# FFT mixing followed by a ReGLU FFN on one core: batch 0 loaded by casting DMAs and folded inside the matmuls of stage 1, with the weights loaded behind it

## The chip, the cores and the metric

The kernel runs on one core of one Trainium2 chip. The metric is the device time of one execution in microseconds (us), the median of several executions. A profiled execution leaves a trace; its span is about 2 us shorter than the device time of the same execution (645.1 against 646.91 us in the kernel before). A program on one core has no second core to compare with, so its clock is read from its own trace.

Engines: PE is TensorE (matmul), PEld its weight load, DVE is VectorE, ACT is ScalarE, POOL is GpSimd, SP the engine that issues most of the DMAs. SBUF and PSUM are the two memories in which the kernel places its tiles: matmuls write to the tiles in PSUM, all other tiles are in SBUF. The granted clock is the share of its full clock at which PE was allowed to run. A dummy matmul is one whose result nobody uses; it only keeps PE busy.

## The reference

```python
X = np.fft.fft(x, axis=1)                 # x: (8, 3008, 256), f32
X = np.fft.fft(X, axis=2).real            # 24064 tokens of 256 features
gate = np.maximum(X @ w_gate, 0.0)        # w_gate, w_val: (256, 1536)
val  = X @ w_val
out  = (gate * val) @ w_out               # w_out: (1536, 256)
```

## The kernel before

The sequence length is split as 3008 = 94 x 32. Stage 1 is a DFT of length 94 over the partitions, one matmul group for each of 16 values `jj`. A shuffle through DRAM turns the result around, and stage 2 is a DFT of length 32 that yields `pq` (two halves, `cs` = 0 and 1) for a block of 512 columns. The feature DFT is never run on the data. It is put into the weights: `pair_w` adds and subtracts the two halves of a weight chunk, and `fold_w` multiplies them in f32 with a table of cosines and sines (`cd`) to give `wc`, `ws` and a scaled copy `wm`. There are twelve folds in all: three column chunks `n`, two weights `i`, two tables `cs`.

```python
def pair_w(n, i, eng):
    lo, hi, up = (wst[i, n, c] for c in range(3))
    eng.tensor_tensor(up, lo, hi, op=ALU.add)
    eng.tensor_tensor(lo, lo, hi, op=ALU.subtract)

def fold_w(n, i, cs, evac="act"):
    ...                                                      # two f32 matmul pairs into ps
    if cs == 0:
        plain(wc[i][:, sl_], ps[:])
    else:
        plain(ws[i][:, sl_], ps[:])
        nc.scalar.activation(wm[i][:, sl_], ps[:], ACTF.Copy, scale=s2[:])
```

After that come 288 steps (8 batches x 3 blocks x 12 columns of 128 of the hidden dimension). A step computes the gate from `pq`, `wc` and `ws`, the value, and their product. The first twelve steps have no output matmuls yet. They therefore have room on PE, and some folds sit between them. The output matmuls of a block run beside the steps of the next block.

Batch 0 comes as f32 through SP, DVE and POOL fold it (`fold_first`: sum and difference of each feature with its mirror feature), and stage 1 then needs two matmuls of 256 columns for a `jj`. The order of the program after the tables is also the order in which each engine works in these traces (the `pq` copy ran behind `pair_w(1, 1)` at 38.26 us in the changed kernel, and ahead of it, at 33.65, when an experiment exchanged the two calls):

```python
for r in (0, 24):
    fold_first(r, 8, ALU.add, dve)
...                                                          # more sums on DVE, differences on POOL
for c0, c1, ev in ((1, 4, "aaa"), (4, 6, "aa"), (6, 8, "ad"), (0, 1, "a")):
    for c in range(c0, c1):
        stage1(0, c, "act" if ev[c - c0] == "a" else "dve")  # 4 matmuls and a copy out of PSUM
    shuffle_out(0, c0, c1)
load_w(1, (1,))
for blk in range(NBLK):
    shuffle_in(0, 4 * blk, 4 * blk + 4)
load_w(2)
...
pair_w(0, 0, dve)
for cs, off in enumerate((o0, o1)):                          # stage-2 table m2: DVE chain and a sine on ACT
    if cs:
        pair_w(0, 1, dve)
        fold_w(0, 0, 0)
        fold_w(0, 0, 1)
    ...
fold_w(0, 1, 0)
fold_w(0, 1, 1)
...
pair_w(1, 0, pl)
pair_w(1, 1, dve)
fold_w(1, 0, 0, "act")
fold_w(1, 0, 1, "act")
...
stage2(0, 0, 0, "act")
rotate(0)
fold_w(1, 1, 0, "act")
stage2(0, 0, 1, "dve")                                       # its copy on DVE releases the first full gate
```

## Time and profile before

| | |
|---|---|
| time | 647.8 us (647.26 to 647.83) |
| span of the profiled execution | 645.1 us |
| PE busy over the span | 96% |
| last stage-1 copy ends | 24.56 us |
| stage 2 starts | 33.26 us |
| first full gate (matmul of `ws` with the second half of `pq`) | 37.37 us |
| first output matmul | 65.09 us |

The page shows where PE is not full. Its second part cuts the span into 40 slices of 16.1 us; a digit is the busy share of PE in tenths, and in the second line the granted clock of PE in tenths of full speed:

```profile
PE   6878999899999999999999999999999999999995
PEclk9699999999999999999999999999999999999999
```

Apart from the eighth and the last slice (8 and 5), only the first four have room, and the second one ran at a low clock. This is the stretch that the change touches. The chain of waits, whose lines give start, length and what, has one piece for the folding of batch 0:

```profile
7.93 10.42 POOL eo L139 x6
```

The windows view by stage follows. The columns are the stretch in us, its length, then busy us and (instructions) of PE, PEld, DVE, ACT and POOL, then the granted clock, the DMA share and GB/s. The four stretches are stage 1 (here from the end of the dummy matmuls ahead of it, after the change from its first matmul), last stage-1 copy to stage 2, stage 2 to the first full gate, and the twelve steps without output:

```profile
9.70:24.57 14.87, 8.35 (x36) 6.09 (x38) 13.60 (x26) 8.15 (x13) 12.93 (x19) 0.65 0.73 220
24.57:33.26 8.69, 7.67 (x25) 2.78 (x21) 7.63 (x19) 4.25 (x9) 3.57 (x5) 0.81 0.80 240
33.26:37.37 4.11, 2.13 (x16) 0.81 (x16) 0.70 (x3) 2.48 (x6) 3.80 (x4) 1.00 1.09 308
37.37:65.09 27.72, 24.29 (x125) 9.23 (x125) 19.35 (x32) 15.52 (x29) 20.21 (x29) 1.00 0.66 123
```

In stage 1, DVE and POOL work for 13.6 and 12.9 of 14.9 us, PE for 8.4 us and at a mean clock of 0.65. The timeline from the end of stage 1 to the first full gate (start, us, engine, line, operation, out<-in, shapes, count, and in brackets the idle time before it and its releaser):

```profile
23.98 0.58 ACT L193 CAST t<-ps 96x512 bf16<-96x512 f32 x1 [2.07 <-PE ps L181]
...
28.95 4.37 PE L282 MATMUL psw<-wst,cd 128*64 128x512 f32 x16 [1.02 <-DVE wst L275]
...
32.26 0.32 POOL L457 COPY seen<-t 1x1 bf16<-1x1 bf16 x1 [4.78 <-DMA t<-Td]
...
33.26 0.40 PE L225 MATMUL ps<-m,t 128*128 128x128 bf16 x4
...
37.37 0.37 PE L518 MATMUL G<-pq,ws 128*128 128x496 bf16 x1 [0.57 <-DVE pq L232]
```

The POOL copy at 32.26 is a marker: it reads one element of the shuffled data and so shows when the shuffle has landed. Stage 2 starts a microsecond later. The last line is the first full gate; PE waited 0.57 us for the `pq` copy.

### The profile page before, as it was taken

The numbers are of one execution on the slowest core, as the hardware profiler recorded it, in microseconds if no ns is written. First come the engines' busy times: TensorE is split into PE (matmuls) and PEld (weight loads), VectorE is DVE, ScalarE is ACT, GpSimd is POOL, SyncE is SP. The second block draws the span as 40 slices with busy tenths as digits, with TensorE's granted clock in tenths as the row PEclk, the third lists the DMA queues.
The fourth block names the chain that finished last, engine by engine and source line by source line (L and its number), as shares of the span: only waits on it lengthen the run. The fifth ranks groups of instructions, "written<-read, shape, count | busy, mean of one in ns | idle before, by whom it ended". The sixth has DMA issues, their size and how long they took to land.

```text
span 645.1 us, 11866 instructions
## 1 busy us (share of the span) xinstructions
PE 618.7 (96%) x4231; PEld 410.4 (64%) x4231; DVE 549.3 (85%) x642; ACT 444.7 (69%) x846; POOL 521.9 (81%) x436
## 2 busy tenths in 40 slices
PE   6878999899999999999999999999999999999995
PEld 3423666666666666666666666676666666666664
DVE  9847888788988988988988897888988898899991
ACT  5455687667677767677777776777677777766660
POOL 9559989999999999999998999898555555556661
PEclk9699999999999999999999999999999999999999
DMA  9694753562735284344723555211512133212114
GB/s 248 197 242 68 173 147 83 153 161 67 207 83 137 43 234 103 106 102 114 195 65 87 121 142 150 59 33 37 156 51 60 46 93 93 67 33 65 32 39 92
DMA packets 35635, 70.72 MB, mean 110 GB/s; under 512 B 6124, under 2 KB 23508, under 8 KB 32244
## 3 DMA queue, kind: packets, MB, share of 16 engines
q1 hardware_dynamic: 32152, 57.92, 34.2%
q0 software_dynamic: 3120, 11.80, 8.0%
q8 instruction: 33, 0.54, 0.4%
q10 hardware_dynamic: 304, 0.25, 0.2%
q14 instruction: 26, 0.21, 0.1%
HBM read 39.77 MB, written 30.96 MB: 110 GB/s over the span
## 4 chain that ended last, share of the span: by engine, by line
PE 82%; DMA 5%; POOL 5%; DVE 3%; ACT 2%; issue 1%; SPq 1%; ACTq 0%; POOLq 0%; DVEq 0%
PE po L581 35%; PE V L532 17%; PE G L524 8%; PE G L518 8%; PE G L517 8%; DMA t<-Td 2%; DMA Td<-t 2%; PE ps L183 2%; POOL eo L139 2%; PE ps L225 1%; PE psw L282 1%; DVE E L539 1%; POOL h L552 1%; SPq L632 1%; DVE h L545 1%
## 5 line engine op out<-in xcount | busy, mean ns | idle before, releaser
L552 POOL TENSOR_TENSOR h<-gm,E 128x992 bf16<-128x992 f32 (+1 forms) x138 | 319.9, 2318 | 87.2 <-DVE E L559 51.7
L581 PE MATMUL po<-wo,h 128*128 128x256 bf16 (+2 forms) x2304 | 326.0, 272 | 0.0
L581 PEld LDWEIGHTS <-h 128*128 128x128 bf16 (+2 forms) x2304 | 231.7, 103 | 106.1
L526 ACT ACTIVATE gm<-G 128x496 f32<-128x496 f32 (+1 forms) x288 | 170.3, 591 | 101.0 <-PE G L524 95.9
L545 DVE TENSOR_TENSOR h<-gs,V 128x1024 bf16<-128x1024 f32 (+3 forms) x150 | 173.7, 1158 | 54.9 <-PE V L532 40.5
L539 DVE SCALAR_TENSOR_TENSOR E<-nb,af,V 128x496 f32<-128x496 bf16 (+1 forms) x276 | 190.2, 730 | 12.3 <-POOL h L552 5.6
L519 ACT ACTIVATE gs<-G 128x497 f32<-128x497 f32 (+2 forms) x288 | 169.7, 589 | 26.2 <-PE G L518 24.1
L559 DVE SCALAR_TENSOR_TENSOR E<-E,V 128x992 f32<-128x992 f32 (+1 forms) x138 | 164.3, 1190 | 0.0
L524 PE MATMUL G<-pq,wm 128*128 128x496 bf16 (+1 forms) x288 | 107.9, 375 | 2.3 <-ACT gs L519 2.2
L518 PE MATMUL G<-pq,ws 128*128 128x497 bf16 (+2 forms) x288 | 107.9, 375 | 0.6 <-DVE pq L232 0.6
L517 PE MATMUL G<-pq,wc 128*128 128x497 bf16 (+2 forms) x288 | 107.9, 375 | 0.0
L532 PE MATMUL V<-pq,ws 128*128 128x497 bf16 (+2 forms) x288 | 85.4, 374 | 3.5 <-DVE E L539 3.4
L532 PE MATMUL V<-pq,wc 128*128 128x497 bf16 (+2 forms) x288 | 85.5, 375 | 0.0
L594 ACT COPY os<-po 128x512 f32<-128x512 f32 x63 | 36.9, 586 | 17.6 <-PE po L581 17.0
L518 PEld LDWEIGHTS <-ws 128*128 128x128 bf16 x288 | 28.2, 98 | 32.6
L193 ACT CAST t<-ps 96x512 bf16<-96x512 f32 x63 | 36.6, 581 | 8.7 <-PE ps L181 6.7
L532 PEld LDWEIGHTS <-wc 128*128 128x128 bf16 x288 | 27.7, 98 | 22.5 <-issue 3.9
L517 PEld LDWEIGHTS <-wc 128*128 128x128 bf16 x288 | 28.2, 98 | 20.3 <-issue 2.9
L110 POOL TENSOR_TENSOR eo<-xla 94x254 bf16<-94x254 f32 x56 | 39.9, 722 | 1.0
L107 POOL TENSOR_TENSOR xla<-xla,xha 94x510 f32<-94x510 f32 x28 | 35.4, 1264 | 2.2
L110 POOL TENSOR_TENSOR eo<-xlb 94x254 bf16<-94x254 f32 (+1 forms) x42 | 33.7, 813 | 0.7
L532 PEld LDWEIGHTS <-ws 128*128 128x128 bf16 x288 | 26.5, 97 | 9.7 <-issue 6.3
(125 smaller groups left out, 380.9 us busy)
## 6 DMA issues: line engine op xcount, KB each, us to landing
out_dram<-os SPq DMA_DIRECT2D x126, 128.0 KB
out_dram<-os SPq DMA_DIRECT2D x86, 64.0 KB
Td<-t SPq DMA_DIRECT2D x7, 768.0 KB
t<-Td SPq DMA_DIRECT2D x7, 768.0 KB
xla<-in_x_dram SPq DMA_DIRECT2D x7, 720.0 KB
xlb<-in_x_dram SPq DMA_DIRECT2D x7, 640.0 KB
nb<-Nd SPq DMA_DIRECT2D x24, 128.0 KB
out_dram<-os SPq DMA_DIRECT2D x39, 48.0 KB
```

The source lines that it names most:

```text
L110: yield eng.tensor_tensor(e1[:, :, o:o + H - 1], x1[:, :, 1:H], free(x1, D - 1, [D, n], [-1, H - 1]), op=op)
L517: nc.tensor.matmul(G[:, ds], lhsT=wc[0][:, fs], rhs=pq[:, 0, ds], start=True, stop=False)
L518: nc.tensor.matmul(G[:, ds], lhsT=ws[0][:, fs], rhs=pq[:, 1, ds], start=False, stop=True)
L519: nc.scalar.activation(pair(t, "gs")[:, t % 2, ds], G[:, ds], ACTF.Relu)
L524: nc.tensor.matmul(G[:, cols], lhsT=wm[0][:, f * 128:(f + 1) * 128], rhs=pqt[b, blk][:, 1, cols], start=False, stop=True, skip_group_check ...
L526: nc.scalar.activation(pair(t, "gm")[:, t % 2, cols], G[:, cols], ACTF.Relu)
L532: nc.tensor.matmul(pair(t, "V")[:, t % 2, cs], lhsT=w[:, f * 128:(f + 1) * 128], rhs=pqt[b, blk][:, min(k, 1), cs], start=(k == 0), stop=( ...
L539: nc.vector.scalar_tensor_tensor(pair(t, "E")[:, t % 2, cols], nbt[b, blk][:, cols], af[:, f:f + 1], pair(t, "V")[:, t % 2, cols], op0=ALU ...
L545: nc.vector.tensor_tensor(pair(t, "h")[:, k, 0, 0:ds.stop - ds.start], pair(t, "gs")[:, k, ds], pair(t, "V")[:, k, ds], op=ALU.mult)
L552: eng.tensor_tensor(free(pair(t, "h")[:], 1024 * (t % 2) + 512 + w - 1, [1024, n], [-1, w]), pair(t, "gm")[:, k, cols], val[:, k, cols], o ...
L559: nc.vector.scalar_tensor_tensor(E[:, :, cols], E[:, :, cols], 2.0, V[:, :, cols], op0=ALU.mult, op1=ALU.subtract)
L581: nc.tensor.matmul(po[0:m, i, :], lhsT=pair(t - f + ff, "h")[:, ff % 2, sg, g * 128:g * 128 + m], rhs=wo[:, ff, :], start=(ff == 0), stop= ...
```

## The change

Its intent is to take the folding of batch 0 off DVE and POOL. The loads of x go through POOL's queue and cast to bf16. The upper rows are gathered in reversed order by an index tile. Stage 1 reads each row forward and reversed and does the folding by accumulation in PSUM: eight matmuls of about 128 columns for a `jj` instead of two of 256. The weight loads start when x has landed. Along with this, tables, folds and copies were reordered. The diff, cut to its core:

```diff
-        for r in FIRST:
-            nc.sync.dma_start(out=t[r // JH][:, r % JH:r % JH + 4, :], ...)   # f32
+            nc.gpsimd.dma_start(out=dst, in_=view(x, r * D, ...))              # f32 -> bf16, lower rows
+            nc.gpsimd.indirect_dma_start(out=dst..., in_offset=...ixf...)      # f32 -> bf16, upper rows reversed
...
-                nc.tensor.matmul(o, lhsT=w1[:, jj, :], rhs=eo[:, jj, :], start=True, stop=False)
-                nc.tensor.matmul(o, lhsT=w1h[:, NB // 2 - jj, :], rhs=eh[:, NB // 2 - jj, :], start=False, stop=True)
+                r0, r1 = (free(v, D - 1, [-1, H - 1]) for v in (x0, x1))       # reversed reads
+                run(o, [(0, H + 1, ce[0], x0[:, 0:H + 1]), (1, H, ce[0], r0),
+                        (1, H, ce[1], r1), (0, H + 1, ce[1], x1[:, 0:H + 1])])
+                run(o, [(H + 1, D, up[0], x0[:, 1:H]), (H + 1, D, up[1], flip[0]),
+                        (H + 1, D, dn[0], r0), (H + 1, D, dn[1], flip[1])])
...
-            nc.scalar.activation(wm[i][:, sl_], ps[:], ACTF.Copy, scale=s2[:])
+            nc.vector.tensor_scalar(wm[i][:, sl_], ws[i][:, sl_], scalar1=s2[:], scalar2=None, op0=ALU.mult)
...
-        (fold_first calls on DVE and POOL)
+        (stage-2 table m2: two chains on DVE with a sine on ACT each, now here)
+        for c0, c1, idle in ((1, 4, 2), (4, 6, 2), (6, 8, 0), (0, 1, 8)):
+            for c in range(c0, c1):
+                stage1(0, c, ("act", "dve")[k % 2])
+            ...
+            warm(idle)                                                         # dummy matmuls
+        for i in range(2):
+            pair_w(0, i, dve)
+            fold_w(0, i, 0, "act")
+            fold_w(0, i, 1, "act")
         pair_w(1, 0, pl)
-        pair_w(1, 1, dve)
-        fold_w(1, 0, 0, "act")
-        fold_w(1, 0, 1, "act")
         ...                                                                    # loads of x of batch 1 and of w_out
+        pair_w(1, 1, dve)
     stage2(0, 0, 0, "act")
     rotate(0)
-    fold_w(1, 1, 0, "act")
     stage2(0, 0, 1, "dve")
...
-    at(0, fold_w, 1, 1, 1, "dve")
     for k in range(4):
-        at(3 + k, fold_w, 2, k // 2, k % 2, "dve" if k % 2 else "act")
+        at(1 + k // 2, fold_w, 1, k // 2, k % 2)
+        at(4 + k, fold_w, 2, k // 2, k % 2)
```

`at(t, ...)` puts work into step t. Before, seven folds run ahead of the steps and five in them; after, four run ahead and eight in them.

## The prediction

> **What bounds it now.** The page has PE busy 96% of the 645.1 us span; the chain of waits gives PE 82%. In the windows view PE is busy 20.0 of 20 us in 80–100 us, and the change does not touch that part. Only the start can move: in the chain the first output matmul stands at 65 us. From timeline and chain:
> - 0–7.9 us: tables on POOL, DVE and ACT while x streams (265 GB/s, last x packet near 14.7).
> - 7.9–18.4: POOL folds batch 0 (10.4 us in the chain).
> - Stage 1 ends with its last copy at 24.57. PE idled from 9.7 to 13.6 but for one matmul, and the granted clock was 0.50 in 15–25: a 256-column matmul took 0.21 us, not 0.11. [...]
> - 24.6–33.3: shuffle through DRAM (landed 32.3) beside six weight folds (1.06 us each at full clock) on PE; stage 2 starts at 33.26, a seventh fold follows, and the first gate matmul that needs both halves runs at 37.37.
> - 37.4–64.8: twelve steps, 1.8 us each without a weight fold and 2.4–2.6 with one.

> **What the change does.** Removes: 24 us of folding of batch 0 (10.6 POOL, 13.3 DVE), the second sine table, three weight folds (3.2 us) before the steps, and the 0.69 us ACT scaling after each fold (now a bf16 DVE op). Adds: stage 1 becomes 128 matmuls of about 128 columns. Four such with new weights took 0.22 us in stage 2, so 7.0 us at full clock, 14 at half (before: 34 matmuls, 7.3 at half). x comes by POOL's queue[...]. A POOL issue took 0.9–1.6 us here, its first packet came 2–5 us after its start, against 1.0 on the sync queue. Casting itself looked free: w_out's cast packets read 1 KB in 60 ns, 270 GB/s over 16 engines. Moves: weight loads behind x; eight weight folds instead of five into the twelve steps.

> **Estimate.** x lands in order: the first two loads near 10 us, the last near 16–17. Stage-1 tables are ready by 9. But the stage-2 sines precede the first stage-1 copy on ACT; their DVE chain (about 25 small ops) ends near 16, and PSUM holds four of eight stage-1 groups until then. The second half of stage 1 runs from 16.5 to 20–23.5, by the clock: last copy about 21.5 (-3). Stage 2 then waits for the shuffle (about 7): 28.3 (-5). First full gate: 30.7 (-6.5), as no fold stands between. Three more folds in the steps give back 1.5–2. Net -4.8, all at the start.

> Predicted 643 us, 80% range 638 to 647.5; faster by over 2%: 3%, within 2%: 95%, slower by over 2%: 2%.

> **What would show it.** Last stage-1 copy at 20–23.5; first full gate at 29–33; the steps in 28–30 us; first output matmul near 60; the stretch after it unchanged within 1 us; clock above 0.5 through most of 10–20.

> **What would make it wrong.** POOL's descriptors late[...], so that x lands after 18; reversed bf16 reads slowing PE (no such read is in this trace); half clock through stage 1 (+3.5 us); the steps with two folds costing over 3.5 us; w_out or batch 1 arriving too late for an earlier loop.

-6.5 us at the first full gate and 1.5 to 2 us given back in the steps make the net -4.8. Of its figures for POOL's queue, the first one is wider in the whole trace of the kernel before: there the first packet came 1.7 to 6.9 us after the start of a POOL issue.

## The result, and the profile after

The changed kernel took 653.8 us (652.86 to 655.09, four runs) against 647.77 us of the kernel before (647.26 to 647.83, four runs): a ratio of 1.0096, with a 95% interval of 1.0076 to 1.0117. It is slower by about 1%, and above the predicted range. A ratio here and below is the mean time of one kernel's runs over the mean of the other's of the same rounds, so it is not quite the ratio of the medians quoted.

| profiled execution | before | after | length of the stretch before | after | predicted for it |
|---|---|---|---|---|---|
| last stage-1 copy ends | 24.56 | 23.25 | 24.56 | 23.25 | 21.5 |
| stage 2 starts | 33.26 | 34.47 | 8.70 | 11.22 | 6.8 |
| first full gate | 37.37 | 38.99 | 4.11 | 4.52 | 2.4 |
| first output matmul | 65.09 | 69.39 | 27.72 | 30.40 | 29.5 |
| end of the span | 645.13 | 651.08 | 580.04 | 581.69 | 580.0 |

(The predicted 29.5 is the old 27.7 and the middle of "1.5–2".) Stage 1 gained 1.3 us, not 3. Each later stretch became longer: by 2.5, 0.4, 2.7 and 1.65 us. The same two lines of the page, after, with slices of 16.3 us:

```profile
PE   7779999899999999999999999999999999999994
PEclk9879999899999999999999999999999999999998
```

The second slice now has a better clock (8 instead of 6), but the third fell from 9 to 7, and a slice further on (the eighth) to 8. The windows view after, for the same four stretches:

```profile
8.81:23.25 14.44, 10.63 (x136) 9.44 (x137) 8.42 (x34) 4.95 (x15) 3.64 (x17) 0.88 0.59 151
23.25:34.47 11.22, 7.89 (x22) 1.96 (x20) 4.94 (x5) 1.76 (x3) 6.51 (x6) 0.85 0.91 297
34.47:38.99 4.52, 1.02 (x12) 0.61 (x12) 3.71 (x5) 1.19 (x3) 4.44 (x4) 0.85 1.06 225
38.99:69.39 30.40, 29.20 (x137) 10.40 (x138) 19.82 (x34) 17.04 (x32) 24.65 (x36) 0.91 0.53 101
```

The first line shows that the aim was met: DVE and POOL fell from 13.6 and 12.9 us to 8.4 and 3.6. Yet the stretch is as long as before. In the second line PE has four folds of 1.06 us to do, where it had six, and takes 11.22 us for them. In the third, PE works 1.02 of 4.52 us. Nothing there is short of engine time, so something is waiting. The timeline after shows for what, first in stage 1:

```profile
14.10 0.31 ACT L40 ACTIVATE sv<-q 128x128 f32<-128x128 f32 x1 [2.08 <-DVE q L39]
...
15.87 0.31 ACT L40 ACTIVATE sv<-q 128x128 f32<-128x128 f32 x1 [1.47 <-DVE q L39]
16.09 1.05 ACT L192 CAST t<-ps 96x512 bf16<-96x512 f32 x2
...
16.42 1.28 DVE L194 CAST t<-ps 96x512 bf16<-96x512 f32 x2
16.70 0.27 PE L162 MATMUL ps<-lo,w 94*96 94x129 bf16 x2 [3.70 <-ACT t L192]
```

The two `sv` lines are the sines of the stage-2 table. They stand ahead of the first stage-1 copy in ACT's order and wait for their chain on DVE. PE had filled the PSUM buffers that it may use and stood idle for 3.70 us, until ACT's first copy freed one. x was not the reason: its last cast packet arrived at 13.17 us (14.74 us before, as f32). The next piece is the folds:

```profile
24.18 2.44 PE L279 MATMUL psw<-wst,cd 128*64 128x512 f32 x8
...
26.66 0.59 ACT L286 CAST ws<-psw 128x512 bf16<-128x512 f32 x1 [0.27 <-PE psw L279]
27.28 0.35 DVE L287 TENSOR_SCALAR wm<-ws,s 128x512 bf16<-128x512 bf16 x1 [2.70 <-ACT ws L286]
27.35 1.40 POOL L272 TENSOR_TENSOR wst<-wst 128x512 f32<-128x512 f32 x1 [13.17 <-DMA wst<-in_moe_w_gate_dram]
27.55 1.75 DVE L272 TENSOR_TENSOR wst<-wst 128x512 f32<-128x512 f32 x1
...
29.35 1.07 PE L279 MATMUL psw<-wst,cd 128*64 128x512 f32 x2 [2.73 <-DVE wst L272]
30.48 0.53 POOL L453 COPY seen<-t 1x1 bf16<-1x1 bf16 x1
31.02 3.52 PE L279 MATMUL psw<-wst,cd 128*64 128x512 f32 x6 [0.60 <-DVE wst L273]
...
34.47 0.40 PE L224 MATMUL ps<-m,t 128*128 128x128 bf16 x4
```

The shuffle had landed by 30.48, but stage 2 started at 34.47, behind the folds in PE's order. After the second fold PE waits 2.73 us for the add of `pair_w(0, 1)`. DVE could have done that add long before, but it stands behind the scaling `wm`, and the scaling waits for ACT's copy of `ws`, which waits for PE's second fold. When DVE comes to it, POOL has just begun its own pair, and DVE's add of the same shape takes 1.75 us instead of 0.68. The last six fold matmuls then take 3.52 us, at half clock (0.50 granted from 30.83 to 34.24). The third stretch:

```profile
35.98 0.68 DVE L272 TENSOR_TENSOR wst<-wst 128x512 f32<-128x512 f32 x1
36.69 1.64 DVE L273 TENSOR_TENSOR wst<-wst 128x512 f32<-128x512 f32 x1
38.26 0.68 DVE L231 CAST pq<-ps 128x512 bf16<-128x512 f32 x1
38.99 0.57 PE L514 MATMUL G<-pq,ws 128*128 128x496 bf16 x1 [2.57 <-DVE pq L231]
```

PE had finished stage 2 at 36.2. DVE first worked through `pair_w(1, 1)`, which nobody needed yet, and only then copied `pq`. The gate waited 2.57 us for that copy.

Last, the late part. In the waits view (engine, line, waited for: us in total, times, longest) the line of `E` for the start of a block reads before (105 to 130 us), then after (109 to 136 us):

```profile
DVE E L539 <- DMA nb<-Nd: 2.7, 1, 2.7
```

```profile
DVE E L535 <- DMA nb<-Nd: 3.3, 1, 3.3
```

Both kernels wait there for a row that goes through DRAM at the end of stage 2 of batch 1. After the change the wait is followed by a stretch at half clock (122.99 to 126.40), which the trace of before has not. Between steps 11 and 36 the two traces run at a constant distance of 4.3 us; at steps 37 to 40 it grows by 2.4 us, falls back to 4.89 by the last step, and what follows the last step's gate (the last output matmuls and the stores) adds 1.06 us.

The granted clock is a part of all this. Up to the last matmul, the stretches at half clock in these two traces last 3.41 us or multiples of it (17.18–20.59, 30.83–34.24, 37.66–44.48, 122.99–126.40; before there was one, 14.22–27.88). In the 3.41 us ahead of each of them PE was not idle: it was busy for 14, 31, 37 and 35% of that time, and for 24% ahead of the one before the change.

### The profile page after: what moved, and what is told of

It reads as the page before. It is cut to its first block, busy times and chain, and to the rows that moved or that the text cites. A ratio compares the mean times of both kernels' runs of the same rounds, so it can differ in the third digit from the quotient of the medians.

```text
span 651.1 us, 12004 instructions
## 1 busy us (share of the span) xinstructions
PE 623.4 (96%) x4294; PEld 413.9 (64%) x4327; DVE 541.1 (83%) x645; ACT 439.5 (68%) x841; POOL 511.9 (79%) x431
## 4 chain that ended last, share of the span: by engine, by line
PE 74%; POOL 11%; issue 3%; DVE 2%; DMA 2%; ACT 1%; POOLq 0%; ACTq 0%; DVEq 0%
PE po L577 31%; PE V L528 15%; PE G L513 8%; PE G L520 8%; PE G L514 8%; POOL h L548 5%; POOL eo L110 2%; PE ps L162 2%; POOL xlb L107 1%; PE psw L279 1%; DMA t<-Td 1%; PE ps L224 1%; DVE E L535 1%; POOL xla L107 1%; DMA nb<-Nd 1%
## 5 line engine op out<-in xcount | busy, mean ns | idle before, releaser
L528 PE MATMUL V<-pq,ws 128*128 128x496 bf16 (+2 forms) x276 | 83.7, 378 | 3.6 <-DVE E L535 3.6
L528 PE MATMUL V<-pq,wc 128*128 128x496 bf16 (+2 forms) x270 | 82.5, 378 | 0.0
L514 PEld LDWEIGHTS <-ws 128*128 128x128 bf16 x288 | 28.3, 98 | 33.0 <-issue 0.5
L192 ACT CAST t<-ps 96x512 bf16<-96x512 f32 x60 | 34.8, 582 | 6.0 <-PE ps L162 4.1
L520 PEld LDWEIGHTS <-wm 128*128 128x128 bf16 x288 | 28.2, 98 | 7.8 <-issue 5.1
```

The costliest lines, as they stand in the source:

```text
L514: nc.tensor.matmul(G[:, ds], lhsT=ws[0][:, fs], rhs=pq[:, 1, ds], start=False, stop=True)
L520: nc.tensor.matmul(G[:, cols], lhsT=wm[0][:, f * 128:(f + 1) * 128], rhs=pqt[b, blk][:, 1, cols], start=False, stop=True, skip_group_check ...
L528: nc.tensor.matmul(pair(t, "V")[:, t % 2, cs], lhsT=w[:, f * 128:(f + 1) * 128], rhs=pqt[b, blk][:, min(k, 1), cs], start=(k == 0), stop=( ...
```

## The experiments

The theory was: (A) the new order makes PE wait in three places, namely the stage-1 copies behind the sines, the second pair behind the first weight's scaling, and the `pq` copy behind `pair_w(1, 1)`. The rivals: (B) it is only the clock, which falls in gaps and would be kept by dummy matmuls; (C) it is contention of DVE with POOL; (D) it is the x path itself, that is casting loads, reversed reads, or the weights' late arrival. The expectations of the first three experiments use other letters: there B is x and the weights arriving late, and C is the cost of steps with two weight folds.

The kernels ran in three sets on three chips. Each set has its own runs of the kernel before (medians 648.4, 647.62 and 648.46 us), and the ratios are to those. The changed kernel ran again only in the third set, so in the other two it can be compared only by way of the kernel before. All kernels gave correct results.

A caution for reading the milestones: the changed kernel's profiled executions differ by up to 2 us in where stage 1 ends (23.25 here, 25.28 in a later one), and the stretch at half clock lies differently there (17.18 to 20.59 us here; in the later one the matmuls of 127 columns took 0.31 us, as in that stretch, from 16.75 to 24.24 us, instead of the 0.22 at full clock). The lengths between milestones are steadier: 11.22, 4.52 and 30.40 us in the first, 11.42, 4.49 and 30.61 us in the later one.

### The `pq` copy ahead of the pair

```diff
-        pair_w(1, 1, dve)
     ...
     stage2(0, 0, 1, "dve")
+    pair_w(1, 1, nc.vector)
```

> The changed kernel with one DVE op pair moved: the add and subtract of the second slice of w_val stand behind the copy of the first stage-2 sine half (pq) instead of ahead of it. Theory A (order on DVE): that pair held DVE from 35.98 to 38.33 us while PE had stage 2 done at 36.2, so the first full gate comes about 2.3 us earlier (36.5 instead of 38.99), PE loses less clock, time 650 to 651.5. Rival B (x by POOL's queue and the weights behind it land too late) and rival C (steps with two weight folds are what costs): no change, 653 to 654.

Measured: 649.18 us (645.67 to 650.14, four runs), ratio 1.0015 [0.9998, 1.0032]; a little better than expected. From stage 2 to the gate it took 2.53 us instead of 4.52. The timeline:

```profile
33.65 0.69 DVE L231 CAST pq<-ps 128x512 bf16<-128x512 f32 x1 [0.70 <-issue]
...
34.39 0.37 PE L514 MATMUL G<-pq,ws 128*128 128x496 bf16 x1 [0.57 <-DVE pq L231]
```

DVE copies `pq` as soon as stage 2 ends, and PE waits 0.57 us, as it did in the kernel before. This place is worth 2 us, and it is shown. The milestone itself moved more (34.39 against 38.99). The rest is not plainly from the edit, for it lies ahead of the moved pair: in this execution DVE's add of `pair_w(0, 1)`, begun 0.25 us ahead of POOL's, took 0.69 us and POOL's 1.56, and the last six fold matmuls ran at full clock in 1.93 us.

### Both pairs ahead of the four folds

```diff
         for i in range(2):
             pair_w(0, i, dve)
+        for i in range(2):
             fold_w(0, i, 0, "act")
             fold_w(0, i, 1, "act")
```

> The changed kernel with both add/subtract pairs of the first weight slices put ahead of the four weight folds on DVE. Theory A: the third fold no longer waits behind the bf16 scaling of the second and behind POOL; PE runs the four folds without its gap of 2.7 us (26.6 to 29.35) and at full clock, stage 2 begins at 30 to 31 (shuffle landing) instead of 34.47, time 649 to 651. Rival B (w_val has not landed before 27 us): the pair just waits at its new place, stage 2 within 0.5 us of 34.5, time 653 to 654.

Measured: 647.28 us (646.8 to 647.77, four runs), ratio 0.9983 [0.9966, 1.0]; better than expected. The timeline:

```profile
24.92 4.16 PE L279 MATMUL psw<-wst,cd 128*64 128x512 f32 x16
...
33.19 0.69 DVE L272 TENSOR_TENSOR wst<-wst 128x512 f32<-128x512 f32 x1 [2.21 <-DMA wst<-in_moe_w_val_dram]
...
35.28 0.57 PE L515 MATMUL G<-pq,ws 128*128 128x496 bf16 x1 [2.14 <-DVE pq L231]
```

The 16 matmuls of the four folds now run in one piece. From the end of stage 1 to stage 2 it took 5.76 us instead of 11.22, and stage 2 starts 0.66 us behind the last fold. The order of DVE was the cause of the gap between the folds. Part of the gain was given back at the next place: DVE came early to `pair_w(1, 1)`, whose weights had not arrived, and held the `pq` copy behind that DMA (stage 2 to gate 5.54 us).

### Both edits

```diff
 (both diffs above)
```

> Both moves. Theory A: first full gate at 32 to 34, time 646 to 648.5, so the loss against the kernel before is gone; the steps from first full gate to first output matmul stay near 30 us or fall to 28 by the clock. Rival C (two folds in a step cost what was lost): the first gate comes earlier but the twelve steps grow, time stays above 651.

Measured: 646.48 us (645.2 to 647.12, four runs), ratio 0.9967 [0.995, 0.9984]. The first full gate is at 33.12 us and the first output matmul at 62.77. With two reorderings of DVE, and nothing else, the change is no longer slower than the kernel before. The steps took 29.65 us, as long as the prediction had them, so the steps with two weight folds are not the unforeseen loss.

### POOL's pair later

```diff
-        pair_w(1, 0, pl)
         pl.tensor_copy(seen[:, 0:1], ...)
         ...                                  # loads of x of batch 1, issue of w_out
+        pair_w(1, 0, pl)
         pair_w(1, 1, dve)
```

> The changed kernel with POOL's add/subtract of the second w_gate slice moved behind the issue of w_out, so that it no longer runs beside DVE's pair of w_val at 27.5 to 31. Theory A, part contention: DVE's two ops fall from 1.75 and 1.64 us to 0.69 each, the third fold starts at 28.3 to 28.9 instead of 29.35 and the fold group ends 1.5 to 2.5 us earlier; but the second slice of w_gate is ready only after 37, which may hold step 1. Time 651.5 to 653.5. Without contention as a cause: the two DVE ops keep 1.6 us.

Measured: 650.24 us (645.94 to 653.61, four runs), ratio 1.0013 [0.9959, 1.0067]; the runs spread by 8 us and the verdict is unclear; the median is a little better than expected. The timeline:

```profile
29.90 0.68 DVE L272 TENSOR_TENSOR wst<-wst 128x512 f32<-128x512 f32 x1
...
30.64 2.66 PE L279 MATMUL psw<-wst,cd 128*64 128x512 f32 x8 [1.67 <-DVE wst L272]
...
36.02 1.34 POOL L272 TENSOR_TENSOR wst<-wst 128x512 f32<-128x512 f32 x1
...
36.28 1.63 DVE L273 TENSOR_TENSOR wst<-wst 128x512 f32<-128x512 f32 x1
```

Without POOL beside it the add takes 0.68 us, and PE's gap before the third fold shrinks from 2.73 to 1.67 us. So of that gap 1.06 us are contention and 1.67 us are order. PE's next gap (0.60 us, before 31.02 in the changed kernel) is gone too, and from stage 1 to stage 2 it took 7.93 us instead of 11.22. The collision then moved to the next pair, whose subtract took 1.63 us beside POOL's add. (Its add took 1.75 us at 34.49, before POOL's pair began; why, no run shows.) That pair still stood ahead of the `pq` copy, and the gate came at 38.58.

Rival C is real. In the folds and before the gate, PE of the changed kernel waits 5.3 us (2.73, 0.60, and 2.57 less the 0.57 that the kernel before waits too), and 2.6 us of that, about half, is DVE being slowed by POOL (1.06, 0.60, and 0.96 in the subtract at 36.69). But it reaches the path only through the order: with both pairs first, all four operations of these pairs took 0.68 to 0.69 us. Which of the two engines took longer differed between the traces: at 27.35 POOL began 0.2 us ahead of DVE, and DVE took 1.75 us instead of 0.68; with the `pq` copy first, DVE began 0.25 us ahead and kept its 0.69, and POOL took 1.56 us, where it takes 1.26 with DVE idle (27.57, scaling on ACT). Who begins first does not settle it in these traces: with the dummies alone, DVE began a subtract 0.03 us ahead of POOL's add (35.90) and took 1.87 us.

### Dummy matmuls in two gaps, nothing moved

```diff
+    def fill(n):
+        pf = borrow("psf")
+        for k in range(n):
+            nc.tensor.matmul(pf[:], lhsT=wk[:, 512:640], rhs=wk[:, 0:512], start=True, stop=True)
         for i in range(2):
             pair_w(0, i, dve)
+            if i:
+                fill(12)
             fold_w(0, i, 0, "act")
...
     stage2(0, 0, 1, "dve")
+    fill(12)
```

> The changed kernel, nothing moved: 12 dummy matmuls put into each of PE's two gaps (before the third weight fold, 26.6 to 29.35 us, and between stage 2 and the first full gate, 36.2 to 38.99). Clock theory: the gaps themselves stay, but the clock no longer falls to 0.5 behind them (it did at 30.8 and 37.7 to 44.5), so the third and fourth folds take 2.1 us instead of 3.5 and the first steps run at full speed; 3 to 4 us of the loss come back, 649.5 to 651, and the runs spread less. If only the waits count and the clock does not: no change, 653 to 655.

Measured: 651.13 us (647.98 to 653.5, six runs), ratio 1.0056 [1.0033, 1.008]. The median is just above the expected range, the spread of 5.5 us did not shrink, and beside the 1.0051 of the changed kernel's later runs no gain in time is shown. In the profiled execution (649.61 us) the clock stayed at 1.0 from 22.56 to 121.55 us; from stage 1 to stage 2 it took 9.64 us instead of 11.22, and the steps took 28.79 us instead of 30.40. The gate still came late, for the waits were as before:

```profile
27.86 2.76 PE L302 MATMUL psf<-wk 128*128 128x512 bf16 x12
...
38.57 0.37 PE L524 MATMUL G<-pq,ws 128*128 128x496 bf16 x1
```

This rejects rival B as the whole: with the clock held through both gaps, this execution is still 2.0 us slower than the median before (647.62 us in the same set, at most 648.64). The clock is a share of the loss (1.6 us ahead of stage 2 and 1.6 us in the steps of this trace), and its falls follow the gaps.

### Both edits, and the stage-2 table behind stage 1

```diff
 (both edits above, and:)
-        for cs, off in enumerate((o0, o1)):       # ahead of stage 1: t2, sin_of, m2
-            ...
         (stage 1, shuffle, weight loads)
         for i in range(2):
             pair_w(0, i, dve)
+        for cs, off in enumerate((o0, o1)):
+            ...
         for i in range(2):
             fold_w(0, i, 0, "act")
```

> Both moves of the third experiment, and the table of stage-2 sines is made after stage 1 (behind the two pairs on DVE) instead of ahead of its first copies. If the copies of stage 1 are what its second half waits for (PE idle 13.0 to 16.7): last stage-1 copy at 18.5 to 20.5 instead of 23.3, shuffle landed by 28, first full gate at 28.5 to 31, time 642 to 645. If the x loads hold stage 1: last copy stays after 22, time 646 to 647.

Measured: 642.91 us (640.2 to 645.5, six runs), ratio 0.9929 [0.9908, 0.9951]. The first three stretches of its windows view, with the columns as before:

```profile
8.00:17.70 9.70, 8.70 (x133) 7.90 (x135) 5.76 (x24) 5.11 (x14) 4.33 (x19) 1.00 0.84 186
17.70:24.20 6.50, 5.09 (x21) 1.88 (x20) 5.85 (x14) 0.31 (x1) 1.30 (x2) 1.00 0.89 275
24.20:28.34 4.14, 1.19 (x11) 0.66 (x11) 2.38 (x6) 2.85 (x7) 2.91 (x4) 0.94 1.01 328
```

Stage 1 now ends at 17.70 us instead of 23.25, with PE busy 8.7 of 9.7 us. The table's place in the order of ACT and DVE, with the half clock behind that wait (17.18 to 20.59), had cost 5.5 us there. The first full gate is at 28.34 us, 10.6 us ahead of the changed kernel's.

### The scaling back on ACT

```diff
-            nc.vector.tensor_scalar(wm[i][:, sl_], ws[i][:, sl_], scalar1=s2[:], scalar2=None, op0=ALU.mult)
+            nc.scalar.activation(wm[i][:, sl_], ps[:], ACTF.Copy, scale=s2[:])
```

> The changed kernel with one part undone: the scaling of each weight fold is on ACT from PSUM again. Theory A (DVE order): without the scaling ahead of it the pair of w_val starts at 24.6, before POOL's pair, and PE's third fold follows the second at 26.6; time 649.5 to 652, close to the second experiment. If only the collision with POOL matters: no gain.

Measured: 649.44 us (646.99 to 652.99, six runs), ratio 1.0034 [1.0009, 1.006]. The four folds run in one piece here too:

```profile
24.20 4.15 PE L279 MATMUL psw<-wst,cd 128*64 128x512 f32 x16
```

From the end of stage 1 to stage 2 it took 5.54 us. This confirms the gap's mechanism from another side: with the scaling off DVE, nothing on DVE waits for ACT between the two pairs. As with both pairs first, `pair_w(1, 1)` then waited for its weights ahead of the `pq` copy (6.62 us idle, gate at 34.62), and the steps took 31.75 us, the first of them at half clock (33.83 to 40.66). In time, beside the 1.0051 of the changed kernel's later runs, no gain is shown.

### The x path alone

The order of weights, folds, table and scaling is that of the kernel before; only the casting loads, the weight loads behind x, the stage 1 with reversed reads, its tables, and its dummies are kept.

```diff
 (against the changed kernel)
-            nc.vector.tensor_scalar(wm[i][:, sl_], ws[i][:, sl_], ...)
+            nc.scalar.activation(wm[i][:, sl_], ps[:], ACTF.Copy, scale=s2[:])
-        (m2 table ahead of stage 1)
+        (m2 table behind stage 1, with pair_w(0, *) and fold_w(0, *) between, as before)
+        pair_w(1, 1, dve)                     # back to its place, with the three folds of n = 1 behind it
+        fold_w(1, 0, 0, "act")
+        fold_w(1, 0, 1, "act")
...                                            # fold_w(1, 1, 0) in stage 2, five folds in the steps, as before
```

> One part of the change alone: x by casting loads and stage 1 folding by reversed reads as in the changed kernel, but the weight folds, their order, their copies on ACT and the place of the stage-2 sines as in the kernel before (weight loads still start behind x). If the new way for x is a gain by itself: last stage-1 copy at 18.5 to 21, time 643 to 646.5. If the loss comes from x (POOL's queue, 128 small matmuls): time 650 or more.

Measured: 641.81 us (641.05 to 643.82, five runs), ratio 0.9923 [0.991, 0.9936]; better than expected. Its windows view, first and last stretch:

```profile
8.00:17.92 9.92, 8.81 (x135) 7.93 (x136) 5.77 (x24) 5.09 (x14) 4.31 (x19) 1.00 0.85 193
...
31.29:59.03 27.74, 24.24 (x124) 9.24 (x125) 19.37 (x32) 15.51 (x29) 20.15 (x27) 1.00 0.72 139
```

The clock never fell below 1.0 from 4.95 to 633 us. The steps took 27.74 us, as before the change (27.72). The first output matmul is at 59.03 us, 6.06 us ahead of the kernel before, and the median is 5.8 us lower. This rejects rival D: the x path is a gain of about 0.8%, and the loss comes from the rest of the change: the order of table, pairs and folds, and the place of the scaling. That the gain is near the 4.8 us predicted for the whole change is chance, since that sum had 3 us from stage 1, where the x path alone brought 6.6.

The version with both edits and the table moved (two experiments back) ran in the same set, at 0.9929. Against it, the x path alone has its first full gate 2.95 us later, but its steps are 1.54 us shorter and the stretch after them 1.3 us shorter. So the rest of the change, three folds moved into the steps among it, bought nothing that these runs show, even with its order put right.

### The changed kernel again

This is the same kernel in the rounds of the next three experiments, so that they can be compared with it on one chip.

> The changed kernel once more, in the same rounds as the three below, for its spread and its clock. If the loss is steady: 652.5 to 655 again, mean granted clock 0.978 to 0.983, the slower runs at the lower clock. If it was a chance of that chip or job: below 651.

Measured: 653.25 us (647.44 to 655.91, six runs), ratio 1.0051 [1.0015, 1.0086]. It varies more than the kernel before (647.11 to 649.6, eleven runs), and roughly with its clock: 655.91 us at a mean granted clock of 0.979, 654.88 and 654.05 at 0.980, 652.44 at 0.983, 648.99 at 0.989, 647.44 at 0.987. Two of the six are below the 651 us of the expectation, and the fastest is as fast as the kernel before. The size of the loss goes with the clock that a run happens to get, from nothing to about 7 us.

### Only the stage-2 table moved

```diff
-        for cs, off in enumerate((o0, o1)):       # ahead of stage 1
-            ...
         (stage 1, shuffle, weight loads)
+        for cs, off in enumerate((o0, o1)):
+            ...
         for i in range(2):
             pair_w(0, i, dve)                     # order of the pairs as in the changed kernel
```

> The changed kernel with the stage-2 sines moved behind stage 1 and nothing else: the order of DVE's pairs stays. Theory: stage 1 ends at 17.8 instead of 23.3, but DVE then makes the sine table (3.6 us) before the first pair, so the folds start at 22 instead of 24.2, their gaps stay, and the first full gate comes at 36 to 37; time 649.5 to 652, so most of the 5.5 us are given back. If the end of stage 1 alone decided the time: 647 to 649.

Measured: 648.92 us (647.74 to 651.1, six runs), ratio 1.0015 [0.9996, 1.0034]; a little better than expected. Stage 1 ended at 17.73 us, yet the gate came at 35.67: from stage 1 to stage 2 it took 12.84 us. So 5.5 us gained in stage 1 shrank to 3.3 us at the gate, because the folds still waited for DVE. With this run the four combinations are complete: neither edit 1.0051 (1.0096 in the first measurement), pairs and copy reordered 0.9967, table moved 1.0015, both 0.9929. With 1.0051 for neither, the two edits simply add up (0.9967 x 1.0015 / 1.0051 = 0.9931); with 1.0096 they would give 0.9887, below the interval of the measured 0.9929. Neither is enough alone to beat the version with both.

### Dummies added to the version with both

```diff
 (the version with both edits and the table behind stage 1, and:)
+    fill(6)
     stage2(0, 0, 0, "act")
+    fill(8)
     rotate(0)
     stage2(0, 0, 1, "dve")
+    fill(4)
```

> The sixth experiment (both moves, sines late) with 6, 8 and 4 dummy matmuls in PE's three gaps between the last fold of the first slices and the first full gate. Clock theory: the window at half clock from 27.9 to 31.3 goes away, the gaps stay; the median falls from 642.9 to 640 to 641.5 and the spread (640.2 to 645.5) narrows to 2 us. If the dummies hold back what follows: 643 or more.

Measured: 644.43 us (638.77 to 645.28, six runs), ratio 0.9915 [0.9883, 0.9947]. This missed. Two of the six runs held the clock (0.997 and 0.998, 638.77 and 640.61 us); four did not (0.989 to 0.992, 644.26 to 645.28 us). In the profiled one, two operations of the table's DVE chain met POOL's pair:

```profile
23.21 1.17 DVE L37 TENSOR_SCALAR q<-t 128x128 f32<-128x128 f32 x1
...
24.41 1.31 DVE L38 TENSOR_SCALAR q<-q 128x128 f32<-128x128 f32 x1
```

They take 0.23 us each alone. The gaps of PE moved with them, away from where the dummies stood. A fixed number of dummies in a fixed place covers a gap only if the gap keeps its place.

### The same, with stage 2 of batch 1 earlier

```diff
-    plan = {0: ((18, 19, 20, 21, 22, 23, 24, 25), 26, 32, (33, 34, 35, 37, 39, 41)),
+    plan = {0: ((18, 19, 20, 21, 22, 23, 24, 25), 26, 31, (32, 33, 35, 37, 39, 41)),
```

> The tenth experiment, and the stage 2 of batch 1 for its first block one to two steps earlier. If the wait of DVE for the row nb at the change from batch 0 to 1 (2.7 us before, 3.3 us after the change) is a fixed round trip through DRAM counted from that stage 2: the wait falls by 1.5 to 2.5 us and so does the time, to 638.5 to 640, and no half-clock window at 113 to 126 us is seen. If the shuffle of batch 1 has not landed two steps earlier: no gain.

Measured: 641.03 us (637.21 to 644.22, six runs), ratio 0.9891 [0.9861, 0.9922]. The wait for `nb` is gone from the waits view between 95 and 125 us. In the same rounds this is the lowest median, but its interval overlaps the previous one's; that the earlier stage 2 alone gains is not settled by these runs. In its trace the lead over the kernel before grows by 2.0 us at step 37 and falls back by 1.5 us up to step 49. The expected 638.5 to 640 us was missed. It beats both kernels.

### The milestones of all runs

The lengths, in us, are of one profiled execution each; the ratios are of all runs.

| run | stage 1 ends | to stage 2 | to full gate | the steps | ratio to before |
|---|---|---|---|---|---|
| before | 24.56 | 8.70 | 4.11 | 27.72 | 1 |
| the change | 23.25 | 11.22 | 4.52 | 30.40 | 1.0096 |
| the change again | 25.28 | 11.42 | 4.49 | 30.61 | 1.0051 |
| `pq` copy first | 23.29 | 8.57 | 2.53 | 29.64 | 1.0015 |
| pairs first | 23.98 | 5.76 | 5.54 | 29.78 | 0.9983 |
| both | 23.28 | 5.43 | 4.41 | 29.65 | 0.9967 |
| POOL's pair later | 25.3 | 7.93 | 5.35 | 29.81 | 1.0013 |
| dummies alone | 24.55 | 9.64 | 4.38 | 28.79 | 1.0056 |
| scaling on ACT | 23.26 | 5.54 | 5.82 | 31.75 | 1.0034 |
| table moved alone | 17.73 | 12.84 | 5.10 | 29.31 | 1.0015 |
| both, and table moved | 17.70 | 6.50 | 4.14 | 29.28 | 0.9929 |
| the same, dummies | 18.49 | 6.33 | 5.87 | 30.59 | 0.9915 |
| the same, stage 2 earlier | 17.74 | 6.63 | 4.10 | 28.44 | 0.9891 |
| x path alone | 17.92 | 9.85 | 3.52 | 27.74 | 0.9923 |

## Why the prediction was wrong

It said 643 us and the kernel took 653.8. The table in the result section lets the 10.8 us be read off by stretch: 1.75 us in stage 1, 4.4 us from there to stage 2, 2.1 us to the gate, 0.9 us in the steps, and 1.65 us after them.

- Right: what bounds the kernel, and that the change acts at the start (4.3 of the 5.95 us between the two spans arise before the first output matmul). Right too was that x lands before 18 us (13.17), and that DVE and POOL are relieved. Last stage-1 copy "at 20–23.5": 23.25.
- The step that failed: "Stage 2 then waits for the shuffle (about 7): 28.3 (-5). First full gate: 30.7 (-6.5), as no fold stands between." Stage 2 did not wait for the shuffle, which had landed by 30.48. It waited for four folds on PE, to 34.47. The prediction has no wait for these folds: by PE's time alone (4 x 1.06 us) they fit into the shuffle, and what feeds them is not in the sum. The second pair stands on DVE behind a scaling that waits for ACT, and so late that it collides with POOL's pair; the half clock behind the gap slowed the last folds. Reordering DVE took this stretch to 5.76 and 5.54 us in two different ways. The gate did not follow stage 2 by 2.4 us either, since `pair_w(1, 1)` stood ahead of the `pq` copy on DVE; moving it brought 2.53 us.
- The move of the scaling to DVE was booked as a saving ("the 0.69 us ACT scaling after each fold (now a bf16 DVE op)"). It is a shorter operation, 0.35 us, but it put a wait for ACT into the engine that prepares the next fold. Undoing it closed the gap of the folds.
- The sines ahead of the copies were seen ("the stage-2 sines precede the first stage-1 copy on ACT") but not priced against the alternative. The estimate took the resulting 21.5 us as the effect of the change. Moving the table brought 17.70 us.
- The clock: "clock above 0.5 through most of 10–20" held in the sense that only 17.18–20.59 was at half. But the new gaps were followed by new half-clock windows at 30.83 and 37.66, in stretches for which the prediction had none. The steps took 30.4 us, a little over the predicted 28 to 30; with dummies in the gaps 28.8 us.
- "The stretch after it unchanged within 1 us" was wrong: it grew by 1.65 us. The `nb` wait and the half-clock window after it are in the trace. The last 1.06 us are not explained: from the last step's gate (the ACT operation at 627.73 us before and 632.62 after) to the end it lasts 17.40 us before and 18.46 after, but 17.42 with the dummies alone and 18.37 with the x path alone, which is fast. The difference lies behind the last matmul, in the stores (7.23 and 8.29 us). It varies from run to run, and no experiment was made on it.

What stays open is the exact split of the loss between order, contention and clock over the whole kernel. The falls of the clock follow the waits, and the position of its windows changes from run to run; the run for contention was unclear in time. For the stretch from stage 1 to stage 2 the profiled executions give a rough split: 11.22 us in the changed kernel, 9.64 with the clock held, 7.93 without the collision and nearly all at full clock, 5.76 with the pairs first. That is about 1.6 us for the clock, 1.7 for contention and 2.2 for the order alone, from one execution each; with the order put right, all three were gone.

## What to carry to other kernels

When work is taken off a path, follow each remaining operation of the new critical engine back through the program order of the engines that feed it. Two folds that cost PE 2.1 us at full clock held it for 7.9 us here (26.62 to 34.47), because a shorter operation, moved to another engine, put a wait into the feeder's queue, and contention (DVE's add took 1.75 us instead of 0.68) and a lower clock (0.50 from 30.83 to 34.24) came on top; with that one operation moved back, all four folds took 4.15 us. Order each engine's queue by who is waited for next, keep the preparation for later behind the copy that is needed now, and test the parts of a mixed change apart: here one part was worth 0.8% and the other parts more than lost it.
